# A gated linear attention with a PReLU MLP: small gate operations and the state's decay on other engines, in a new order

## The chip, the core and the metric

The kernel runs on one core of a Trainium2 chip. The core has five engines, each with an instruction queue of its own that it works through in order: TensorE (PE in the profile) for matrix products, VectorE (DVE) and ScalarE (ACT) for elementwise work, GpSimd (POOL) for elementwise work on SBUF, and SyncE (SP), which here issues the transfers between the memory (HBM) and the on-chip SBUF. Matrix products land in PSUM. The metric is the time of one execution in microseconds (us); a change of the kernel is judged by the median of several runs.

## What is computed

The first half is an attention with a complex gate. Each of 4 x 8 heads keeps a state of 48 x 48 complex numbers, which turns and shrinks at every token by a gate per row and takes in the product of key and value; the output reads it with the query. The second half is an MLP with a PReLU on the 3072 tokens.

```python
def _attn_ref(q, k, v, a_re, a_im):              # q, k, v, a_re, a_im: (4, 8, 768, 48)
    mag = np.sqrt(a_re * a_re + a_im * a_im)
    scale = np.minimum(mag, 0.999) / (mag + 1e-06)
    a_re_n, a_im_n = (a_re * scale, a_im * scale)
    for t in range(S):
        ar, ai = (a_re_n[:, :, t, :, None], a_im_n[:, :, t, :, None])
        new_re = ar * S_re - ai * S_im
        new_im = ar * S_im + ai * S_re
        kv = np.einsum('bhd,bhe->bhde', k[:, :, t], v[:, :, t])
        S_re, S_im = (new_re + kv, new_im)
        y[:, :, t] = np.einsum('bhd,bhde->bhe', q[:, :, t], S_re)

def _moe_ref(x, w_in, w_out, alpha):             # x: (3072, 384), w_in: (384, 2048)
    h = x @ w_in
    g = np.maximum(h, 0.0) + alpha * np.minimum(h, 0.0)
    return g @ w_out
```

## The kernel before

The gate of a token is split into a magnitude (the decay) and a direction (the phase). With phases multiplied up along the tokens, keys and queries can be turned once and the state needs only real decays; the decays of a block of tokens are multiplied up in a tree.

**Gates.** `gates(g, b, c0, c1)` does this for batch `b` and the chunks `c0` to `c1` of 128 tokens. There are nine calls, in the list `GATES`: batch 0 in three (1, 2 and 3 chunks), batches 1 to 3 in two of three chunks each. They are numbered g = 0 to 8; the "first gate" is g = 0, "gate 1" and "gate 2" are the other two of batch 0. Rows are the 384 pairs of head and column, as 3 groups of 128 partitions. A call loads the gate (L255), makes the magnitude and its inverse (L263 to L323), the decays (L380) and their tree of products (L396, halving each time; a memset at L383 clears its end), and stores the decays to HBM (L401). The phases are multiplied up in three levels: seven products inside groups of eight tokens (`product`, L416 and L418, on 128x576 and 128x288 elements, later on smaller ones), seven products inside groups of eight of those (the same lines, on 128x72 and 128x36 for three chunks, 128x48 and 128x24 for two), and then the **recurrence**: one product for each of six (or four, or two) remaining blocks, on only 12 and 6 columns, from the value carried over from the gate before (`run`, `carry`, L454 to L468). ScalarE copies the factors between the levels (`three`, L444 and L446). Then the offsets are worked back down (L477, L480), brought to length one (L486 to L492), and multiplied into all tokens by VectorE (L507, L510). The phases are stored to HBM (L502, L512).

The choice of engine for the small steps is made by `tiny`: VectorE in the first gate, GpSimd in the others. `small(k)` and `on(k)` use it for products of up to 80 columns and VectorE for wider ones. For the recurrence `tiny` is set to VectorE in all gates (L454, L455) and set back after it (L468).

**Weights.** The MLP's weights come as 64-bit numbers and are brought to 32 bits in 16 pieces by `to_f32`: ScalarE reads a piece (L588 to L592), GpSimd clips it (L596), VectorE shifts and adds (L598, L600).

**Units.** `unit(u)` does one chunk of one batch, 24 in all. It needs keys and queries (L657, L659), the phases (`PP`, L665) and the decays (`T`, L672), gathered from HBM. VectorE turns keys and queries (L742, L744). Then six levels of halves (1, 2, 4, ... 32 tokens) follow: TensorE multiplies keys by queries (`meet`, L759), VectorE multiplies both by the decays of the next level (`step`, L797), ScalarE copies halves together (L820, L836) and masks results (L773), VectorE too (L782). TensorE transposes the keys (L868), makes the sums of key and value (L880) and the outputs (L900). The **state** `St` is taken along in two halves of 64 tokens: it is multiplied by the decay and the new sum is added by VectorE (L918). In the units 0 to 3 the multiplication is one VectorE instruction of 96x384 (L910), in later ones eight ScalarE instructions of 96x48, one for each head (L916). The state is read by the queries (L930), and the chunk's result goes to HBM (L944, L949).

**MLP.** Groups of one or two chunks are loaded back (L962) and go through `features` (L978, ReLU on ScalarE L985, PReLU on VectorE L987) and `outputs` (L997); the last three groups go through a form with fewer products (`late_features`, `late_outputs`, L1097 to L1172).

**Order.** All of these are Python generators. The string `ORDER` holds one letter for each step: A to I are the gates 0 to 8, J and L the loads of units and values, K spread copies of the values, M start values and weight loads, N and O the weight pieces, P to m the units 0 to 23, n the loads of the MLP, o the MLP, p and q its late form. `plan.run(ORDER)` takes the next step of the task that a letter names, and so writes the queues of all engines in this order; nothing is reordered later. A step waits on its engine for what it needs, and all that stands behind it in the queue waits too.

Of the kernel before, what the change touches and what calls it, by code (L numbers as in the profile page):

```python
# [27 lines left out]


ORDER = (  # L30
    "AABBJAMAJAAAAAAAAAAAJAAMAAAABAJAAAAAABAAAMMMAALALBABAABAABAAANAAAABALAAKOBLNABMNNKAAOMNKABNKBLAALBBK"
    "AOOALABBNABAKAABAKAONMAAKANNAAAABMAOLBAKBOKABABKAAAABLAABANBAAAAOABABABABAKAAKANAAAAANKANBKANAAAOONA"
    "BABLBBNBCBCBKBJBJBBBNBBBOOBCBBBBOBBBCPBOPPJMLLKKBCLCJPCPMOOBBOPPBKOPBBCMKBPNLJBBPPJBCBPNBBCPPNNPBBPK"
    "PJCMBBBCPCPCCPOPBBBBBPOPPBPBOBBMBOBCCCBBBLPBPPPPCPBCCBBPCBPBCPCBOPCPNPOLCCCCDDJCCPCNNNNNCOLCOPLCOOJP"
    "JCPPPCLCDOKCDCNJDCQPPPPCDLMODPNDQMDCNDNKPQJLCQQDLCQNNLQCLOCDQCCCQLCCMDCJDDNQLJOLOOCCCnCJQQCCJDDODQOC"
    "LDKOoJoOoQJDOOQCoCQRDooooCQDLLRQJoQKCooCQQQQQJDMoKCRQQQKoCKNRRQRCNCQOoCQRoQNCRNQCoCoORMQKCoCDCoCoRQo"
    "QLooRQLooCCCCDoLRQoRDLCooRCLoOoCoLRoRJCQCLoooooOQQLQRDCCLoQQCoQRDRDoDNLooLooCCRRCRLRRRLRoooooRoCRKLo"
    "oooooQOOCCCQLooooRooRCDCKoooooDNQDRDRNRRDNJREOoNEDJDNNJoDJRoDLRLDoRDRRRJDoDRoJNDSJDDoDREoooooSDNEJDK"
    "SEDLSESDoSRRRooRESDLLoODonoSSDoSDoooJSTSDELSJoSDoLoLooooSSDoLDDoSLLoooSLTSJSSSoooooSJEooooLoTSLDSLDE"
    "oSJTJooooSoTSTEoKEJooSoSoDTooEDooSTTDSoEEoSTSSEoLELTToLSLoooooSoLDSLELDLSooSoooSoTLSDooSDTSSSoSooKDE"  # L40
    "oLDoooooJEoDDDJooDoTToLoDDDToLELoooooTUoJTDDDDLDTTEKTTJToooooTUDLoDEJoooooUKDoTTnToooJoUEoDToUoTUEoD"
    "UoooETUoEDUDEoEDDTEoKoDooTDoTTLooLoDDooooDLoLooooDLoLoToooDoULoLEULoTLooUUoTEoLUoUJoUFoTTooFTULoTToT"
    "EUoUTTETUUUULUULUoooooEUoVUEoooooUVVUJoEFJoooooJEUoEJUUEUoUUEoLFULoEoJVoELUoFVUJJooLoVEoUKFUVEVLUoEV"
    "UKEoLooooUEVVoUEEoVEooooVoJWVFELVLVoEJooooLoEVVEnEoVJFELoooooLVEWoVELLVVVVFLVLoooooVVVEWJoEJoooWoFKW"
    "EVWJoEWVoFFoooVooooJoEWWEooooFEoEEWVEVWEEVEFVEFVWLVWoLEXLELWEoELoooooLoWWLVFLWEEEEELooooooLoFEWVLEWL"
    "KEEVVVLWWoWWLWVVWoooooVoFVVLWVoEEooWoEWFoWJoFoJoEEWoooJEFooFWEWWEEWJWoLELoWooooEooFWEXLoWLXJJoooXWoF"
    "ooooWWXWXWGoFWXJWLoooooLXXoGoXWWLooooXFoFoFXFoXFFooXooXXoYooGoonoXLooJGYoJXXoLFGXLXLXFXXLXGXLLoooooo"
    "XoGFFLXooooooFXFoGJoooYJXoJoGFKoFXYFoXFXXFXXFXoYXLYoLYJoLYoXXXJYFLGXLFoooooYLXXXXooooXYGoLFoFKYoYGFY"
    "FJoooJoFYYoFLZoFKoGLYFLGoooooJYFZFYLoJYYoFYLYYYJZYFJooooooLZYFGZFLYZLoJZGFooYoYoZoFFZoFFGYoYZYYYYFoZ"
    "oLFYLoFGYLooLFoFFLFYYoYLFGZYLZYYooYYGGFoYFFLFZoFLFoFFoLaoJFFJoooZZoLFGZLJGanoooooGFLFoooZZooZZZFooGZ"  # L50
    "ZLFZGZLFJoooZoGFoZaGFoFoooGZGFoZoaoFZZFZZZZoFFLaoaLFLLFLooooooFoZLoooZaJooLoaLoGaLooooGoaHoHZZaLZGoa"
    "LZaooJGaLoLoGJoaaoaoZZZZoooaZoGaKHGoooaLaoHKGoGHoooooGaoaHaaJaaaJboHoooaooGaoHaGbbKJaoaHaGaooaLGLoHL"
    "ooLGboGbLGoLabJGooooGoLHHGbbLoHbLaGJaobbJooKoGHbGJooLHobLGbabLaabaaGoaLooooGbbLoGLoGbJGoHJooobJGcboJ"
    "obbGbbJbbobGoHoobobocoobobJoHooobGcbbbHbbccLconbHLGcboLooGLcGJcGGLbHGLGcLoGLoooooobcbGoKGcGbGcobobcb"
    "bLGoGHbdoLoGGGHodGoJJooooccKoGcoLoKGHGLHLGoooccocccLGoJoHdLGHJGcoJcooooocoHdGHccGGdoHdcGGooooocoGGoc"
    "GooocoocKcGcccocGodcLoLLKocccooocLddoLocodooodHooHIoIdLdodLoJcoooLHoLoddoJHdoLcooooHdILdoHcLoHLddILo"
    "cIooooooeLdKdodIddddJHJoooododJHoIdHeodIdHdddHLooJHoLoHoeLHoILdJoIHeLHLoooodooeeoeHoLLeoHeLoooHHodLH"
    "oeHLodJoedoHJIeIHLeoLdeIoHKoLedoHneoHHdHeddodIKoooooILeeoeeeeoJIoooJoIHJeeeeoKeoIJHoJfHooeoeooHeIeHf"
    "IeeeeIIofLLoHIJoooeoLHofHHLoeHHfHJIfLfLoLHeeeffKeooooLeofeeeoLoHLHHHoooHfeIfofHHHoofHLoogJHJHfLoHfoo"
    "oooKHIoLHoooLoHIfHJIooKgoIfoffffIffHffHooooJHoLooIoofofgofHogofooooHoooIHfHoJfHffffHgLgLoogLoHofLogg"  # L60
    "oLIoLfoooLgoJooLffoILgfILgfgofJofIfgooggoooIoffogLLoooooLIgJgoggggLoJggIJgooogoIgoIogIogooIogIhgIggg"
    "ghhJJnJoLoLhoJggoLhIgILggoooLhIIghLIghIoghIogoLhhIILIohJILoooooohILihoIhJhLILooooJohhoILiIIoJJIhLJoo"
    "ooooiLooooihIhIoihhiohohJhhoiooIhhoohIoIiihIohioohIiIIIohIIohIIjhhhoLLoIIIhLoIjhoLoILiiLiIoLILhhhIiL"
    "hiIooooLohioIhhhLoIoooIpohoLoIiLiLiioiiLiiJiooooJIioJioIoooioiIoiIIiiiiiijLiJLLjiiioooLooooJIonjjIoo"
    "jILooooJijjooooLijiLoLooooojoLjoJjooLjLoLojjoLoiLoioooijoLoojJojooJjjjjjoJjjJokoJopjojooojojokojkjjk"
    "jjokjLokoLkLokLokojJokjLLLoLkoooooojJkokLjkLjLooLkkoLjkjLojoooojlkjokjkkkkLkkkoooookokoJooolJkokooko"
    "okkkkkoLLolJooJoklJokJoooLooLokJlolLklLkLkookpokkkokoLolloJoooloLoLomlJooolloloolooooomolooooLolLLmL"
    "noooooolLmlomlmlllllooolpooololooomlopooolmmooooomoloomlllllmLmoLmLomomolomolooopooomomllommlollomml"
    "oloomooooooLoooLooomomLoLooLooooloooooLmqLooLoooLooLooooLolonooooomoooooooooooooooooooooooooooopoomo"
    "moooooooomomomoomoomomoopooommomoqmqmqmmmqqmoqqqoooqoooooooqoqqoqooqoqqoooooqqqqooqooqoooooqqoqqoqoo"  # L70
    "qooooooooooqqoooooqqoqqoqooqoqooqoooqqooooqoooooqoqqoqooqoqqooqoqoqqqooqooooqqoooooqoqqoqooqoqooqooq"
    "oqoqooqoqoqoooqqqoqqonoooooooooqqqoqooooooooqoqqqoooooooooooqoqqqoqoqoqqoooqoqqoqooqoqoooooooooooooo"
    "qqoqqoooooooooooqooqoqooooqoqqqoqooqoqooooooooooooooqoqqqoooooooooooqoooooooqoqqoqooqoqqooqoqoqqqoqo"
    "ooooooqqqoooqoqqoqooqoqooooqoqoqooqoqoqoooqqqoqqoooooooooooooqqoooqoooqoqqoqqoooooooooqoooooqqoooqoq"
    "qoqqoooooooooooooooooqooooooooooooqoqqooqooooqoqqqoqooqoqoooooooooooqoooooooooooooqqqoooooqooooqoqqo"
# [1185 lines left out]
```

## Time and profile before

| what | us |
|---|---|
| median of 3 runs (lowest, highest) | 834.2 (831.7, 834.34) |
| the profiled execution | 834.89 |
| its span, first to last instruction | 833.2 |
| TensorE busy in it | 685.4 |
| VectorE busy | 691.2 |
| ScalarE busy | 502.7 |
| GpSimd busy | 249.5 |

The profile is one execution. "Busy" is the time in which an engine worked on an instruction of its own; a wait is put down to the instruction that released it. A group of instructions is given by line, engine, operation and shape: partitions x elements. The page cuts the span into 40 slices of 20.8 us and gives the busy share of each in tenths.

### The profile page before, as it was taken

The numbers are of one execution on the slowest core, as the hardware profiler recorded it, in microseconds if no ns is written. First come the engines' busy times: TensorE is split into PE (matmuls) and PEld (weight loads), VectorE is DVE, ScalarE is ACT, GpSimd is POOL, SyncE is SP. The second block draws the span as 40 slices with busy tenths as digits, with TensorE's granted clock in tenths as the row PEclk, the third lists the DMA queues.
The fourth block names the chain that finished last, engine by engine and source line by source line (L and its number), as shares of the span: only waits on it lengthen the run. The fifth ranks groups of instructions, "written<-read, shape, count | busy, mean of one in ns | idle before, by whom it ended". The sixth has DMA issues, their size and how long they took to land.

```text
span 833.2 us, 27790 instructions
## 1 busy us (share of the span) xinstructions
PE 685.4 (82%) x11680; PEld 542.5 (65%) x11680; DVE 691.2 (83%) x1151; ACT 502.7 (60%) x1243; POOL 249.5 (30%) x341
## 2 busy tenths in 40 slices
PE   0001316859999999899999999999999999999997
PEld 0001315646777667667777777776777777899997
DVE  6978989999999889899998999997887585556574
ACT  8848777557657767776876589554755645311121
POOL 7457454651503110233043121402300000323432
PEclk9999755979999999999999999999999999999999
DMA  7794885696678559547975779678476631201000
GB/s 210 224 274 121 251 233 163 194 217 162 154 226 195 149 145 261 152 123 214 247 177 156 233 165 208 179 193 189 96 204 146 158 90 36 61 2 39 1 20 20
DMA packets 186597, 130.98 MB, mean 157 GB/s; under 512 B 74728, under 2 KB 176872, under 8 KB 186088
## 3 DMA queue, kind: packets, MB, share of 16 engines
q1 hardware_dynamic: 186472, 129.20, 58.5%
q8 instruction: 92, 1.51, 0.8%
q14 instruction: 33, 0.27, 0.1%
HBM read 100.82 MB, written 35.71 MB: 164 GB/s over the span
## 4 chain that ended last, share of the span: by engine, by line
PE 62%; DMA 13%; DVE 11%; SPq 4%; ACT 4%; POOL 4%; issue 2%; DVEq 0%; ACTq 0%; POOLq 0%
PE ps_o L997 18%; PE ps_h L978 16%; PE ps_m L1172 6%; PE ps_lv L759 4%; PE ps_h L1097 3%; PE ps_y L1097 3%; PE ps_y L900 3%; PE ps_kv L880 2%; DVE KQ L797 2%; PE ps_y L930 2%; DVE gate L507 2%; DMA T<-decs 2%; DMA ysc<-T 2%; DMA VL<-in_v_dram 1%; DMA g_sb<-in_w_out_dram 1%
## 5 line engine op out<-in xcount | busy, mean ns | idle before, releaser
L978 PE MATMUL ps_h<-xT,w_in_sb 128*128 128x256 f32 (+1 forms) x960 | 227.8, 369 | 2.8 <-DMA xT<-ysc 1.8
L997 PE MATMUL ps_o<-w_out_sb,g_sb 128*128 128x384 f32 x576 | 224.7, 505 | 5.2 <-DVE g_sb L987 5.0
L978 PEld LDWEIGHTS ps_h<-xT,w_in_sb 128*128 128x128 f32 x960 | 173.0, 196 | 54.9 <-issue 3.2
L797 DVE TENSOR_TENSOR KQ<-KQ,T 96x1024 f32<-96x1024 f32 x120 | 148.8, 1241 | 25.4 <-PE ps_lv L759 18.1
L997 PEld LDWEIGHTS ps_o<-w_out_sb,g_sb 128*128 128x128 f32 x576 | 101.8, 191 | 45.6 <-DVE g_sb L987 7.6
L985 ACT ACTIVATE g_sb<-ps_h 128x256 f32<-128x256 f32 (+1 forms) x160 | 58.0, 362 | 84.7 <-PE ps_h L978 84.1
L759 PE MATMUL ps_lv<-WQ 96*32 96x32 f32 x2304 | 34.9, 204 | 81.7 <-DVE WQ L742 63.0
L416 POOL TENSOR_TENSOR gate<-gate 128x72 f32<-128x72 f32 (+1 forms) x56 | 43.1, 770 | 177.6 <-ACT gate L446 166.1
L759 PEld LDWEIGHTS ps_lv<-WQ 96*32 96x32 f32 x2304 | 26.6, 116 | 101.2 <-DVE WQ L742 63.4
L987 DVE SCALAR_TENSOR_TENSOR g_sb<-g_sb,al,ps_h 128x256 f32<-128x256 f32 (+1 forms) x160 | 71.4, 446 | 20.6 <-ACT g_sb L985 20.4
L1160 POOL TENSOR_TENSOR sums<-g_sb 128x128 f32<-128x128 f32 x48 | 21.9, 476 | 182.0 <-DMA VL<-in_v_dram 109.0
L916 ACT ACTIVATE St<-St,T 96x48 f32<-96x48 f32 x288 | 68.7, 325 | 6.1 <-DVE St L918 6.1
L820 ACT COPY WQ<-KQ 96x1024 f32<-96x1024 f32 x48 | 50.0, 1042 | 23.2 <-DVE KQ L797 23.2
L596 POOL TENSOR_SCALAR top<-top 128x768 f32<-128x768 f32 x16 | 42.6, 2668 | 28.4 <-ACT top L588 26.1
L900 PE MATMUL ps_y<-A,VL 64*48 64x64 f32 x2304 | 42.2, 222 | 8.3 <-issue 6.6
L477 POOL TENSOR_TENSOR gate<-gate,runs 128x252 f32<-128x252 f32 (+1 forms) x16 | 21.0, 1311 | 86.4 <-ACT runs L446 60.5
L507 DVE TENSOR_TENSOR gate<-gate 128x1152 f32<-128x1152 f32 (+2 forms) x36 | 44.3, 1263 | 2.9 <-POOL gate L492 2.7
L416 DVE TENSOR_TENSOR gate<-gate 128x576 f32<-128x576 f32 (+3 forms) x70 | 45.3, 647 | 1.3 <-ACT gate L446 0.4
L900 PEld LDWEIGHTS ps_y<-A,VL 64*48 64x48 f32 x2304 | 39.3, 123 | 10.4 <-issue 9.6
L836 ACT COPY W<-KQ 96x512 f32<-96x512 f32 x48 | 30.8, 642 | 23.7 <-DVE KQ L797 17.4
L759 PE MATMUL ps_lv<-KQ,W 96*32 96x32 f32 x1536 | 24.6, 205 | 24.3 <-ACT W L836 24.0
L773 ACT ACTIVATE A<-ps_lv,columns 128x64 f32<-128x64 f32 x144 | 37.7, 338 | 9.5 <-PE ps_lv L759 9.1
...
## 6 DMA issues: line engine op xcount, KB each, us to landing
...
```

The source lines that it names most:

```text
L416: on(4 * k).tensor_tensor(out=m, in0=w[:, 1::-1].unsqueeze(2).to_broadcast([P, 2, 2, k]), in1=pairs_of(u), op=ALU.mult)
L507: TT(out=m[:, a], in0=U5[:, 1 + a], in1=turned(off3, o)[:, a].unsqueeze(1).unsqueeze(3).to_broadcast([P, L // 2, nb, 2]), op=ALU.mult)
L759: nc.tensor.matmul(t[64 * i + j:64 * i + j + HC // 2, p], lhsT=keys(n, g), rhs=queries(n, g), start=True, stop=True)
L797: nc.vector.tensor_tensor(out=x, in0=x if x0 is None else x0, in1=m, op=ALU.mult)
L820: nc.scalar.copy(z.rearrange("p i n t -> p i (n t)").rearrange("p i (m h) -> p m i h", h=h), bass.AP(tensor=KQ.tensor, offset=KQ.offset + ...
L900: nc.tensor.matmul(o, lhsT=Vp[h][64 * i:64 * i + 64, s, e_ * D:(e_ + 1) * D], rhs=a, start=False, stop=False)
L916: nc.scalar.activation(St[:, n], before[:, n], AF.Copy, scale=T[0:D2, n, TL - 4 + s:TL - 3 + s])
L978: nc.tensor.matmul(p, lhsT=w_in_sb[:, f // 2, kk, f % 2 * P:(f % 2 + 1) * P], rhs=x_of[m][:, kk], start=(kk == 0), stop=(kk == NK - 1))
L985: nc.scalar.activation(gt, p, AF.Relu, scale=-1.0)
L987: nc.vector.scalar_tensor_tensor(out=gt, in0=gt, scalar=al_1[:, f:f + 1], in1=p, op0=ALU.mult, op1=ALU.add)
L997: nc.tensor.matmul(sums[0], lhsT=gt[:, c * P:(c + 1) * P], rhs=w_out_sb[:, f], start=(f == 0), stop=(f == NF - 1))
L1097: nc.tensor.matmul(o, lhsT=lhs, rhs=rhs, start=(at in (0, 5)), stop=(at in (4, 8)))
```

## The change

Three assignments to engines are changed, and the string that sets the order is another one.

- `tiny` is VectorE for the gates 0, 1 and 2 (all of batch 0), and GpSimd for the gates 3 to 8.
- The recurrence no longer goes to VectorE by itself: it is made by the engine that `tiny` names, so by GpSimd in the gates 3 to 8.
- The state is multiplied by the decay on ScalarE in all units; the branch with VectorE's L910 is never taken.
- `ORDER` holds the same steps in another order.

```diff
 ORDER = (
-    "AABBJAMAJAAAAAAAAAAAJAAMAAAABAJAAAAAABAAAMMMAALALBABAABAABAAANAAAABALAAKOBLNABMNNKAAOMNKABNKBLAALBBK"
+    "AABBMMAAAAAAAJAAJAAJAAAAAAAABAAAAAAABAAMMMMAAABABAABAKAABAKANAAAAABAKANBKNNAABOMJBAAAOANOOANBMAKNAAK"
...
-        tiny, tiny_engine = (DVE, nc.vector) if g < 1 else (POOL, nc.gpsimd)
+        tiny, tiny_engine = (DVE, nc.vector) if g < 3 else (POOL, nc.gpsimd)
...
         t = yield from three(ends, blk[:, :, Rn - 1], 2 * rows, t, (R["run"],))
-        here, here_engine = tiny, tiny_engine
-        tiny, tiny_engine = DVE, nc.vector
         t = yield tiny(10, t, *[("carry", g - 1)] * (not first))
...
             done["carry", g] = yield tiny(10, t)
             tiny_engine.tensor_copy(carry, run[:, :, :, nr])
-        tiny, tiny_engine = here, here_engine
         t = yield from three(runs.rearrange("p r (t n) -> p r t n", t=NK), run[:, :, :, 0:nr], 2 * rows, t)
...
-            if u < 4:
+            if u < 0:
                 k_ = yield DVE(H * D, known, takes=(R["St"],))
```

Counted over the whole kernel: VectorE has 1109 instructions in place of 1153, ScalarE 64 more of L916, GpSimd 382 in place of 346; those of TensorE and the 756 transfers of SyncE are the same.

More of the change, by code (lines that the diff above doesn't have):

```diff
@@ L30 @@
 ORDER = (
-    "AABBJAMAJAAAAAAAAAAAJAAMAAAABAJAAAAAABAAAMMMAALALBABAABAABAAANAAAABALAAKOBLNABMNNKAAOMNKABNKBLAALBBK"
[L32 to L75, printed above, removed]
@@ L76 @@
-    "qooqoqqooqoqqqqqqqqqqqqqqqqqqqqqqqqqqqqqqqq")
+    "AABBMMAAAAAAAJAAJAAJAAAAAAAABAAAAAAABAAMMMMAAABABAABAKAABAKANAAAAABAKANBKNNAABOMJBAAAOANOOANBMAKNAAK"
+    "BOKAOAANLAKOALANNBKABLAAAOAKBKOOAAMLAAAKABAAMAABLAAALAAAABAABAABAABAABAAAAAAKBABAAABABANBNBBNONBONNC"
+    "BCOJBNOLBLOOBLBNJBBBBBCBOPCCBPPJMLJJBKNCMBNLBPCBBPCBOCBBBPPCNNPBMBCCJKCBPLCKBPPBCOBCCBCBBOOOBPMBLPPB"
+    "BCLPKBCCKBBBPLJBPKBBBBPBKBBCKPKBPNBPBBBPBBPBPPBPBPPPBPPBPBBCKPBBPNBPKPCNPONLCLNNCCOPDCNJCDOPJPJCCCNC"
+    "LNPPPJCPOMCNCJQOOCNNQJPDCCDLOPCPDQJDQQQLODMQDPQQCDQMDPQQJOQNLOQOOKLQLDDKQODCOnJOLOJLDDQRQLoOOLCoLDoD"
@@ new lines @@
+    "KQoLooJoQoLoDQJQQQMQQooooKCoQDCJCoQCoooooDDQCRoQCRDCRoooooQRCNQoDRONCoooCRoNooCRRCooooQQNNCQCoRLoLCR"
+    "LCoooooRCDCLoCQCLCooRCDoKCoRoLoLRRLCCCCLooooooCMCLCCoooooQKCRCLCLCoCQRLDRCDooLCDLCDRCRoRDRRCRCRRQQRC"
+    "OCRCCoCCRQOCRQQOoCQoQRCCRJRRRQCOOCDCQRLNRLDNKoNDNRRoooREDNNEDoLRDoJRORJDJooooDoJNoRDLNDLDODEnooooJDJ"
+    "SELDSDDEDJSDREJSSRSLoESDLLoooLDSSoDLoDESDoJTLSSDELSJSDoKoooLSSDoJDoDSDoooTDSoSoooLoSSKDSDSJDSSTDJoSK"
+    "ooSoSooTDESJDToTEEDSEoooooSDDoDSEEDooDTDEoooSToDSDSSoDEoLLoooTJSLEoDLDSoooooLTLKoSSSTLoooooTSETDDDDD"
@@ new lines @@
+    "LSoSSSooooTSDooDooooTTooDooooToJDoJooooULoTEEoTLEooJUoonoLTTDTTToELoooooLEToDTooLoTLoUToJoDEUoooooUE"
+    "JUETKEETDDDoJEoooooUoooToDTTKTUUTDUoooLoLDoLUTLooooDoLUULDoLooooDoULoLooooLoUULoTLUTLLoooooUJEUFoETT"
+    "TooEooUUUTTTUTToTFoEUUEUoooUoUEoEoVEooUoUooUoEUVVJJUUUUooLELFUUJoEoLFVoEJUFVJJoEUJVoooooLUEVoFVLUULE"
+    "EUooooFEUVoELooooEVVoEoEFVJELoVooooJEVWFEVnoJVoELLooooEoLVVEEoLVEJoooooKEWVEEVoEWJEJoooooWELVWEVWoLV"
+    "LVFVVVooVoVoooEoFEJFWoEooVoVooEWWoEEVEoWEFVVVEWVFFWLWXKVLWLLoooooEoEVELEWoVLEoooELooKEoLEWELELFFFVWE"
@@ new lines @@
+    "LoLooVVooVoVLFVoEVWVEWVEWFFLLoEEWWWJWWooooooJWWEoWJFJooooEJooWoEWooJEoFooEoWoEWWWoEWWXoKoWXoWooooLFL"
+    "FLoXooooJoFWLoFXFGoXFLWXLWGooLXXoWoXWoWWWoWYXFoooXXoLXooXXonoLXGLFJGoooooXJXFoLXXXLXoGFLYJoooooooFJX"
+    "GXXLLFGooooXooFXFoGFFoooooooGFooXoFoFXooooFJXFJGFXFoXFXYFXXLooJYFoXFKYFXYFLoFYFLooLYoFLYFooFXXLXFYFo"
+    "LXXoXGXXoYXoKYoYGLFooYoFFJFoYYFoFJZFoGLYLFoGLoooooFJZFYJYoYYLFoKYYoooYFYJZoFYYLoGLZoZLYZKoZGFJJoooYF"
+    "KZoFYFoGZoYFGFoFFYYoYZYYoLFLoYLZoFaZYLZFoLZoLFLoYFZZLFoooYoFLYZooYLFoYoFYLGZoZLYFaGYYZZZZGLLGLoooooo"
@@ new lines @@
+    "FFZoJZZZFJZGJoooooZoFZoooZFFZZZZZFoLLoFoJooaFLooooaJoGoLZaonGaZooLaoLoHaoaLoZZHoGZGGLZGZGGaoooLaoGaZ"
+    "LGZaoJaoJoZaaGoooooGHZoLaoHGoooaaGoLGoooaaaoaaLoLaGHooooGoaJHaoJaoJGHooaoGoaboHoaGoaHbbJJaaaaooHLLoJ"
+    "oGoGLboGbLGoKHbJHLooooobLGbaaHGKbGoLobLbGoooGLoGbKoGoLaoLGbboGHHLGboLaobaGaoaaLobbaGoKGobLGGHGoooobG"
+    "bGJoGbbbGJobbbcbGooobobGHobGooboJcoGJbooGbHGbbbbcoGLLobcGJoHboJoLHLGGbbbcJocGGboKbGbLbGLocGbobcocooH"
+    "cJoJcdLGHGLoooooccdJoHGLcnoGLLooooooccoLcGLHLJoooooocdoJcKHdJoooGccdGccdGcocLHcoGHocodcHooooHGoHocoG"
@@ new lines @@
+    "cooocoGGoccGcccoLcoLoGLocHGLooodLdcccooLodLoLooodHIocdIdLodLoLodcdJHoooocodccocLoHooddHodddddodoLoHL"
+    "HoLdIJHooodoHJodeoIdHodoooHoIoHoedoIdddddHILHneHLHHJoooooeoHdLIHeHeLHedHLLHLHodddHLHooooHeeooooHKHoe"
+    "HILLooooeoJIHoLeoedJHoodHJdeHodLoeJeoLoIIddeLHoIooooooHHeHoeHIIHJooHeoHLIJoIoJeHeoeJeeeeKfeHoJfJHooo"
+    "eoeooHHeoHHoHeeHeHeeoLeHLIoeLoofLoHLoIHfJLeLHooeeffoLfIIeHeoeoffoeefoeHLgfooooJgoooofofIJIooofoKoLon"
+    "oILoooffKoHoILofLooooJgooHoKIgfIofIgLIgHHffffffLfooooKHoJfogIfJoKggooofoHfoofoHoJHffffffoLgfLoLoHoLo"
@@ new lines @@
+    "gLfoLHLoooogHgfLgfLofgLfogILfgffLoIoooooooofgIoJgLgggggLggIJIJoooooogIoKgooIogIohgoogIoghhJggggIooLI"
+    "LogJoIoJIgJghLoIghgJogLIooogLoIhoILoIIghoIhgoIoLhILoohhJIoiIoLJhILLihILoLoooooohohILhIJJooooIhhoLIoI"
+    "JhoIIiIooooooohiIJhIiIhhhJoIhhohooIhhIohIIoIIoIhihoiIIhIoIihoIhhIhhihoLILoihLooLjoLIhhhiLIioLIhiohoI"
+    "LhihhoIIhoLioiLojLoLiJoooooLoIioiLooLiiiiiJioiIIoJioiJIoioioooIijiiiiioLoIIIoLoLjiLooooiIoLoLjjJoiiL"
+    "jiIiioooijiiiojooooLojJLoooojoJoLjoJjoojJoJojjJoLojLoLooooLjLjojjjjojjokJjnooooJokojokjooojojokokoko"
@@ new lines @@
+    "jkjkjjjjkjojLkLoLookLjoJkokLjkLjLjoojkLokLojokLjojolLLoookokookkkkjokLolLokLkJpJoookokookokpoookkkkk"
+    "kkoLkolLoLnlJooooooLkoJoLoooJooLlJlklJkollpkkkkkokLooooooolLLmlJJoooooololLmLoooLloLoooooollolooooLm"
+    "LmoooooomllmllooloollplllooloolomlmmoooooomlopmlloooooolllllmLmLolllLmlLlloooLmoLooomoooomooonlooooo"
+    "ooopooooooLmmLomoLooLoLooLoooLooLmoooooomolmoqooooooomommooooopoooooooooooopooomomoooooooooooooooomo"
+    "moooooooomomomoommmooooomooomomoqmqmqmmmqlqmqqqqooooqooqqqoooooqoqqqooooooooqoqqooooqoqqqooooqoqqoqo"
@@ new lines @@
+    "oqooooooqooqqoooooooqoqqoqoooooooooooooooooqonqqqoqooqoqooqoqoqqqqqqqqoqoqqooooooqoooqoqqoqoqooqooqo"
+    "oooqoqooqqooqooqqqoqqoooooooooooooooqqoqoooqqoqoqqoooooooooooooooooqoqqoqooqoqoqqoooooqqoooqooqqoooq"
+    "oqqqooooooooqoqoqooooqooooqoqqqoooooooooooooqoqooooqoqqoqqoooooooooooooooooqoqqoqooqoqooqqqoqoqqqoqo"
+    "oqqooooooooqoqoooooooooqooooqoooooooooooooooqqqooqooqooqooqqqqqqoqqoooooooooooooooooqqqqqoqqqqoqqoqo"
+    "oooooooqoqqqooooqooqoooqoqqoqooqqoooooooooooooooqoqooooooooooooooooooqoqqoqooqqooooooooqqqoooqooooqo"
@@ L79 @@
+    "qqqoqooqoqooqoqqqqqqqqqqqqqqqqqqqqqqqqqqqqq")
 class Ring:
```

## The prediction

> **What bounds the kernel now.** I read the page's first two parts first, then busy time by stage, then who VectorE waits for, then single instructions of GpSimd.
>
> ```profile
> span 833.2 us, 27790 instructions
> PE 685.4 (82%) x11680; PEld 542.5 (65%) x11680; DVE 691.2 (83%) x1151; ACT 502.7 (60%) x1243; POOL 249.5 (30%) x341
> PE   0001316859999999899999999999999999999997
> DVE  6978989999999889899998999997887585556574
> ```
>
> TensorE and VectorE have almost equal work, but not at the same time: TensorE is nearly empty in the first five slices and full from about the ninth on, VectorE is full from the second slice to the 27th. The table by stage gives it in numbers (columns: stage, its length, busy time and count of TensorE, weight loads, VectorE, ScalarE, GpSimd, then clock and DMA).
>
> ```profile
> 14.00:240.00 226.00, 108.04 (x2368) 85.45 (x2368) 206.42 (x338) 152.75 (x280) 113.35 (x98) 0.87 0.72 202
> 240.00:380.00 140.00, 131.78 (x2397) 97.94 (x2396) 124.96 (x184) 102.65 (x259) 28.82 (x45) 0.99 0.67 174
> 380.00:640.00 260.00, 256.77 (x4827) 193.06 (x4826) 235.55 (x334) 172.62 (x480) 54.63 (x77) 1.00 0.73 187
> 640.00:834.00 194.00, 188.78 (x2093) 166.02 (x2091) 118.00 (x274) 63.06 (x200) 43.35 (x96) 1.00 0.19 50
> ```
>
> From 380 us to the end TensorE is idle for 3.2 + 5.2 us, partly because the last slice is cut short. So the time is made of TensorE's work, which the change leaves alone, and of its idle time before 380 us: 14 + 118 + 8.2 us. In that lead-in VectorE is busy for 206.4 of 226 us, so what is worth something is VectorE's work ahead of the early units and its waits there. The waits of VectorE between 14 and 240 us (total, times, longest):
>
> ```profile
> DVE top L598 <- POOL top L596: 7.1, 3, 3.8
> DVE gate L507 <- POOL gate L492: 2.7, 1, 2.7
> DVE g_sb L987 <- ACT g_sb L985: 2.2, 4, 1.0
> DVE WQ L742 <- DMA PP<-phs: 1.7, 1, 1.7
> ```
>
> Of its 19.6 us idle, 9.8 us are GpSimd's fault: the weight pieces (L596) stand in the same queue as the small gate operations and are late. Why those operations take long is seen in the second gate's chain (start, duration):
>
> ```profile
> 51.76 0.28 POOL L416 TENSOR_TENSOR gate<-gate 128x48 f32<-128x48 f32 x1
> 52.12 0.23 POOL L418 TENSOR_TENSOR gate<-gate 128x24 f32<-128x24 f32 x1
> 52.44 0.29 POOL L416 TENSOR_TENSOR gate<-gate 128x48 f32<-128x48 f32 x1
> 52.80 1.16 POOL L418 TENSOR_TENSOR gate<-gate 128x24 f32<-128x24 f32 x1
> 54.04 2.50 POOL L416 TENSOR_TENSOR gate<-gate 128x48 f32<-128x48 f32 x1
> ```
>
> The same form takes 0.28 us, and 2.50 us once VectorE's 1.2 us rotations (L742 at 52.65, L744 at 53.91) run beside it.
>
> **The change, part by part.**
>
> *Small operations of gates 1 and 2 to VectorE.* VectorE has no row for most of these sizes; its neighbours (128x48 at 0.208, 128x24 at 0.184, 128x96 at 0.255, 128x192 at 0.355, 128x288 at 0.476 us) bracket each within 0.05 us. Gate 1: 14 products 2.7, decay ends (L396) 0.6, L477 and L480 1.1, L488 to L492 0.9: 5.3 us. Gate 2: 3.0 + 0.6 + 1.4 + 1.0 = 6.0 us. VectorE gets 11.3 us more before 240 us. GpSimd loses about 22 us of gate 1 (rows 5.7, 4.2, 4.4, 5.3 and small ones) and 19 us of gate 2 (a seventh of 131 us, the rows of seven like gates). With that the 16 weight pieces of 2.67 us stand alone in GpSimd's queue, so I take the waits of 7.1 and 2.7 us as gone. If that cover is wrong, because ScalarE brings the pieces late (GpSimd waited 26.1 us for L588), they stay: bounds 0 and 9.8 us, and I take 9.8, since the causes named were L596 and L492 themselves.
>
> *State times decay.* Eight VectorE instructions (L910, mean 0.599) go: 4.8 us less. ScalarE gets 64 more of L916 at 0.325: 20.8 us, between about 80 and 240 us, where it is busy for 106.6 of 160 us (127.4 then). Queued behind them are ScalarE's copies for the units (L820, L836), for which TensorE waits already. The multiplication needs only the earlier state and the decays, so it can run before the new sums are there; where it can't, a half costs 8 x 0.325 - 0.6 = 2.0 us more. In the trace TensorE waits directly for the state's sum (L918) two times, 6.0 us. Bounds: 0, and 8 halves x 2.0 = 16 us; I take 1 us, nearer to the lower end, as six of eight halves had nobody waiting.
>
> *The recurrence of gates 3 to 8 to GpSimd.* VectorE loses per gate 6 x 0.171 + 6 x 0.165 and a copy or two of 0.245, 2.3 us; 13.6 us in six gates, 2.3 of them before 240 us. GpSimd has no row of 12 or 6 columns. Its 128x12 decay row is 0.208 us alone, its 128x36 product 0.594 us on average and up to 1.25 when it collides, so 12 operations cost from 2.5 to 15 us; I take 7. Behind them in GpSimd's queue stand only the same gate's L477 to L492 and the next gate's memset and L396. On ScalarE the copy L444 to `runs` waits, and in VectorE's queue L507. What hides the chain is VectorE's other work between a gate's last large product (L418, 128x288) and its first L507. Summed from the mean rows in the program order of each kernel, scaled by 691.2/749.8 because neighbouring rows overlap, that cover is 49, 36, 37, 40, 40, 34 us before and 40, 34, 35, 37, 38, 27 us after for gates 3 to 8. The chain is 14 products 9.5 (7 x 1.36), recurrence 7, tail 6.4, ScalarE's hops 3.2: 26 us. It fits, in gate 8 by nothing. I cost it at 0.
>
> The Trainium skill (SBUF — State Buffer, Who interferes with whom) says that a VectorE instruction with two SBUF inputs and a GpSimd instruction that reads SBUF shut each other out for the whole instruction. The 0.28 and 2.50 us above agree; by that rule each of the 12 could wait out a whole rotation, which is the first rival.
>
> *The order.* All 756 transfers of the SP queue remain. Gate 1's decay store goes from the 37th to the 41st place, behind gate 0's phases, some 2 us by issues of 0.4 to 0.6 us; gate 1's phases (L512) from 75th to 76th, unit 1's gather of them (L665) from 80th to 83rd. Unit 1 meets its phases with 11 us of VectorE rows between, against about 10 us from L510 to the gathered tile before: just in time, 0. For VectorE I summed the rows ahead of each unit's first rotation (L742): scaled, they grow by 1.6 us for unit 1, 0.5, 8.9, 6.9, 3.7, 5.2, 4.0, 1.7 for units 2 to 8, then shrink by 1.4 (unit 9), grow by 2.0 (10), shrink by 3.5 (11). These sums already hold the three parts above.
>
> *The sum.* VectorE reaches a unit earlier by the 9.8 us of waits less that growth: unit 3 by 0.9 us, 4 by 2.9, 5 by 6.1, 6 by 4.6, 7 by 5.8, 8 by 8.1, 10 by 7.8. TensorE's idle time ends to grow somewhere between unit 6 and unit 10, so it can shrink by about 6 us. Less the 1 us of ScalarE: 5 us. The profiled execution took 834.9 us (span 833.2 and 1.7 around it); 834.9 - 5 = 829.9. Its time lies 0.7 us over the median of the runs, 834.2, so I say 829.
>
> **The rivals.** *The GpSimd chain becomes the wait (slower).* Place: L507 of gates 4, 5 and 8. With the colliding prices (14 products 13.4 as in gate 3, 12 operations at 1.0, tail 9.8, hops 3.2) the chain is 38 us against 34, 35 and 27 us: 4 + 3 + 11 us of VectorE standing still, and behind L507 stand L987 and the units, with two `ps_h` buffers of cover, so perhaps two thirds reaches TensorE, 12 us: 829 + 12 = 841 us. It decides when an operation of the recurrence costs over about 0.7 us. For it: many of the rows at 1.2 us. Against: gate 8's products ran at 0.26 to 0.32 us.
>
> *ScalarE becomes the bound of the lead-in (slower).* Between 80 and 100 us it is busy for 16.1 of 20 us; 16 instructions of unit 0 make 21.3. If half of the eight halves pay 2.0 us and the copies behind lose as much again, 16 us less the gain: 834.2 + 16 - 6 = 844 us. Against: 20% of the stage stays free.
>
> *Nothing to measure.* The waits on GpSimd are replaced by waits for transfers, whose share is 0.72 in the lead-in (the gather of decays at 99.5 us took 6.6 us): unit 3, which gains only 0.9 us, then sets the rest, 834 us. That the change does not do what it says can be ruled out: the counts of the rows follow the text.
>
> **How the numbers follow.** What a measurement here can tell from no change is about 0.3%, 2.5 us. Forecast 0.48 (its own range 821 to 833), GpSimd's chain 0.22, ScalarE 0.15, nothing 0.15. Faster: 0.44 of the forecast and 0.02 of nothing, 0.46. Same: 0.04 + 0.10 + 0.02 + 0.02 = 0.18. Slower: 0.20 + 0.13 + 0.03 = 0.36. The range goes down to 834 less all of the 9.8 us and half of the 8.2 us idle from 240 to 380, 820, and up to both slower cases, 846.
>
> **What would show it.** Right: between 14 and 240 us no wait of VectorE for L596 or L492 over 1 us in total, VectorE busy there by some 4 us more, TensorE's idle time before 380 us down from 140 to about 135 us, L507 without waits. Wrong: waits of L507 for L492 of several us at gates 4, 5, 8; waits of L918 or of the units' matmuls for ScalarE that grow by more than 5 us; or VectorE's gaps filled by DMA waits at L742 and L797.

## The result and the profile after

The changed kernel took 822.98 us (median of 4 runs, 821.21 to 826.72), the kernel before 833.93 us beside it (4 runs, 831.70 to 834.34): a ratio of 0.9856, 95% interval 0.9821 to 0.9892. It is faster by 11 us; 5 us were forecast. The same kernel on another chip gave 0.9864 (0.9820 to 0.9907; run e11 below). The chips differ by up to 0.5% (the kernel before took 833.9, 835.0, 837.0 and 838.4 us on those used), so runs are compared here by their ratio to the kernel before on the same chip, and traces by the times inside them. The profiled execution of the changed kernel is one of its slower ones, 826.7 us.

In the changed kernel the lines behind the recurrence are numbered 2 or 3 lower: L742 is now L739, L797 is L794, L916 and L918 are L913 and L915, L987 is L984, L507 is L504.

From the first two parts of the page after the change:

```profile
span 825.0 us, 27851 instructions
PE 694.1 (84%) x11680; PEld 548.3 (66%) x11680; DVE 684.1 (83%) x1107; ACT 519.3 (63%) x1307; POOL 268.2 (33%) x377
PE   0001439859999999998999999989999999999997
DVE  5999999999998999896989988978777786455574
```

VectorE's row of nines now holds from the second slice to the 12th; before, the third, fourth and sixth slices were at 7 and 8. Over the whole kernel VectorE works 7.1 us less, ScalarE 16.6 us more, GpSimd 18.7 us more. By stage (columns as in the prediction's table of stages):

```profile
14.00:240.00 226.00, 122.41 (x2492) 96.62 (x2493) 217.96 (x375) 174.58 (x363) 78.41 (x67) 0.93 0.74 207
240.00:380.00 140.00, 133.86 (x2470) 99.85 (x2469) 125.05 (x153) 102.38 (x263) 53.98 (x75) 0.98 0.73 186
380.00:640.00 260.00, 257.35 (x4812) 192.23 (x4811) 222.14 (x284) 174.29 (x480) 84.36 (x115) 0.99 0.69 178
640.00:834.00 194.00, 180.49 (x1911) 159.64 (x1909) 113.33 (x273) 56.91 (x179) 42.83 (x96) 0.99 0.17 44
```

Between 14 and 240 us VectorE is idle for 8.0 us in place of 19.6, and TensorE gets 124 more of its instructions done. VectorE is busy for 11.5 us more there, not for the 4 us of the prediction's signs: by 240 us it has come further in its queue, to 375 instructions in place of 338. GpSimd's load in that stage fell by 35 us. VectorE's longest waits there (in total, times, longest):

```profile
DVE g_sb L984 <- ACT g_sb L982: 2.3, 3, 1.9
DVE St L915 <- ACT St L913: 0.7, 1, 0.7
DVE gate L380 <- ACT gate L373: 0.5, 1, 0.5
DVE KQ L794 <- ACT WQ L817: 0.5, 2, 0.3
```

The view lists no wait for GpSimd any more (it leaves out waits of up to 0.15 us); before there were 9.8 us of them.

TensorE's busy time is no measure of progress here. Two traces of the changed kernel show it: for about the same work before 380 us (4960 and 4948 instructions) TensorE was busy for 256.3 us in this one and for 245.8 us in e11's, because the same product takes longer in some stretches. L897's 64x64 product took 308 ns on average between 140 and 160 us in this one, at a granted clock of 0.70, and 218 ns in e11's, at 1.00. The row of the clock does not tell it everywhere: between 100 and 120 us it says 0.50 before and 1.00 after, yet the 96x32 product (L759, now L756) took 244 ns in both. The start of each unit's first rotation (L742, now L739) is a better measure. From the traces, in us; the last row is e11, whose chip is 0.5% slower:

| unit | 1 | 2 | 3 | 4 | 5 | 6 | 7 | 8 | 10 | 12 | 16 | 23 |
|---|---|---|---|---|---|---|---|---|---|---|---|---|
| before | 103.64 | 130.86 | 177.02 | 188.27 | 216.57 | 247.74 | 265.00 | 286.90 | 352.37 | 409.51 | 510.85 | 668.66 |
| after | 98.09 | 119.56 | 172.33 | 181.85 | 209.92 | 240.49 | 257.73 | 275.39 | 339.89 | 401.03 | 499.06 | 659.36 |
| earlier by | 5.6 | 11.3 | 4.7 | 6.4 | 6.7 | 7.3 | 7.3 | 11.5 | 12.5 | 8.5 | 11.8 | 9.3 |
| forecast for VectorE | | | 0.9 | 2.9 | 6.1 | 4.6 | 5.8 | 8.1 | 7.8 | | | |
| e11, earlier by | 5.0 | 10.7 | 3.7 | 5.7 | 4.7 | 5.1 | 5.0 | 8.8 | 9.3 | 4.9 | 7.6 | 6.8 |

### The profile page after: what moved, and what is told of

Its sections match the earlier page's. It is cut to its first block, busy times and chain, and to the rows that moved or that the text cites. A ratio compares the mean times of both kernels' runs of the same rounds, so it can differ in the third digit from the quotient of the medians.

```text
span 825.0 us, 27851 instructions
## 1 busy us (share of the span) xinstructions
PE 694.1 (84%) x11680; PEld 548.3 (66%) x11680; DVE 684.1 (83%) x1107; ACT 519.3 (63%) x1307; POOL 268.2 (33%) x377
## 4 chain that ended last, share of the span: by engine, by line
PE 69%; DVE 11%; DMA 10%; ACT 3%; issue 2%; POOL 2%; SPq 2%; DVEq 0%; POOLq 0%; ACTq 0%
PE ps_o L994 21%; PE ps_h L975 20%; PE ps_m L1169 6%; PE ps_lv L756 5%; PE ps_y L1094 4%; PE ps_h L1094 4%; PE ps_y L897 4%; PE ps_y L927 3%; PE ps_kv L877 3%; DVE KQ L794 3%; DMA VL<-in_v_dram 2%; DMA T<-decs 2%; PE ps_kt L865 2%; DMA gate<-in_a_im_dram 1%; DMA KQ<-in_q_dram 1%
## 5 line engine op out<-in xcount | busy, mean ns | idle before, releaser
L994 PE MATMUL ps_o<-w_out_sb,g_sb 128*128 128x384 f32 x576 | 228.0, 510 | 2.5 <-DVE g_sb L984 2.5
L794 DVE TENSOR_TENSOR KQ<-KQ,T 96x1024 f32<-96x1024 f32 x120 | 149.2, 1244 | 28.4 <-PE ps_lv L756 19.5
L756 PE MATMUL ps_lv<-WQ 96*32 96x32 f32 x2304 | 34.5, 204 | 79.1 <-DVE WQ L739 63.2
L756 PEld LDWEIGHTS ps_lv<-WQ 96*32 96x32 f32 x2304 | 26.4, 116 | 98.9 <-DVE WQ L739 63.6
L984 DVE SCALAR_TENSOR_TENSOR g_sb<-g_sb,al,ps_h 128x256 f32<-128x256 f32 (+1 forms) x160 | 71.3, 446 | 24.7 <-ACT g_sb L982 22.7
L913 ACT ACTIVATE St<-St,T 96x48 f32<-96x48 f32 x352 | 83.8, 323 | 3.9 <-DVE St L915 3.8
L416 POOL TENSOR_TENSOR gate<-gate 128x72 f32<-128x72 f32 x42 | 24.2, 575 | 148.9 <-ACT gate L446 146.1
L416 DVE TENSOR_TENSOR gate<-gate 128x576 f32<-128x576 f32 (+5 forms) x84 | 50.7, 604 | 1.1
L897 PE MATMUL ps_y<-A,VL 64*48 64x64 f32 x2304 | 44.7, 229 | 7.5 <-issue 5.3
L897 PEld LDWEIGHTS ps_y<-A,VL 64*48 64x48 f32 x2304 | 41.7, 129 | 9.1 <-issue 6.5
L396 POOL TENSOR_TENSOR gate<-gate 128x72 f32<-128x72 f32 (+2 forms) x18 | 19.1, 1059 | 79.4 <-DVE gate L396 78.5
L941 ACT COPY T<-ps_y 48x256 f32<-48x256 f32 x96 | 31.8, 365 | 18.4 <-PE ps_y L927 17.6
L833 ACT COPY W<-KQ 96x512 f32<-96x512 f32 x48 | 30.7, 640 | 19.5 <-DVE KQ L794 11.4
L504 DVE TENSOR_TENSOR gate<-gate 128x1152 f32<-128x1152 f32 (+2 forms) x36 | 42.9, 1219 | 0.1
L756 PE MATMUL ps_lv<-KQ,W 96*32 96x32 f32 x1536 | 24.1, 204 | 21.3 <-ACT W L833 21.3
```

The costliest lines, as they stand in the source:

```text
L416: on(4 * k).tensor_tensor(out=m, in0=w[:, 1::-1].unsqueeze(2).to_broadcast([P, 2, 2, k]), in1=pairs_of(u), op=ALU.mult)
L756: nc.tensor.matmul(t[64 * i + j:64 * i + j + HC // 2, p], lhsT=keys(n, g), rhs=queries(n, g), start=True, stop=True)
L794: nc.vector.tensor_tensor(out=x, in0=x if x0 is None else x0, in1=m, op=ALU.mult)
L897: nc.tensor.matmul(o, lhsT=Vp[h][64 * i:64 * i + 64, s, e_ * D:(e_ + 1) * D], rhs=a, start=False, stop=False)
L984: nc.vector.scalar_tensor_tensor(out=gt, in0=gt, scalar=al_1[:, f:f + 1], in1=p, op0=ALU.mult, op1=ALU.add)
L994: nc.tensor.matmul(sums[0], lhsT=gt[:, c * P:(c + 1) * P], rhs=w_out_sb[:, f], start=(f == 0), stop=(f == NF - 1))
```

## The experiments

The string of letters fits any mix of the three edits, as each step stays one step whatever engine it goes to. So the parts were taken apart: A is the small operations of gates 1 and 2 on VectorE, B the recurrence of gates 3 to 8 on GpSimd, C the state's multiplication on ScalarE in all units. Ratios to the kernel before on the same chip, with 95% intervals. A difference of two of them is known to about 0.004 or 0.005 only, 4 us:

| edits | old order | new order |
|---|---|---|
| none | 1 | 0.9962 (0.9930 to 0.9993), e1 |
| A | 0.9952 (0.9925 to 0.9980), e4 | 0.9886 (0.9845 to 0.9927), e9 |
| A, B | 0.9887 (0.9855 to 0.9918), e8 | 0.9878 (0.9847 to 0.9909), e6 |
| A, C | 1.0021 (0.9992 to 1.0050), e10 | 0.9863 (0.9832 to 0.9895), e5 |
| B, C | | 0.9943 (0.9914 to 0.9972), e3 |
| A, B, C | 0.9966 (0.9931 to 1.0001), e2 | 0.9856 and 0.9864, the changed kernel and e11 |

### e1: the new order alone

```diff
 ORDER = (
-    "AABBJAMAJAAAAAAAAAAAJAAMAAAABAJAAAAAABAAAMMMAALALBABAABAABAAANAAAABALAAKOBLNABMNNKAAOMNKABNKBLAALBBK"
+    "AABBMMAAAAAAAJAAJAAJAAAAAAAABAAAAAAABAAMMMMAAABABAABAKAABAKANAAAAABAKANBKNNAABOMJBAAAOANOOANBMAKNAAK"
...
```

> The new order with the engines as they were before. Theory A (the gain comes from gates 1 and 2 leaving GpSimd's queue): the waits of VectorE for GpSimd before 240 us stay or grow beyond the 9.8 us of the kernel before, since the new order leaves less VectorE work beside gate 1's chain; 836 to 848 us. Theory O (the order itself is the better one, whatever the engines): 821 to 827 us, TensorE's clock and busy time in 100 to 140 us as in the changed kernel.

Measured 833.4 us against 835.0, ratio 0.9962. Neither theory: the order gives a little without the edits, and far less than the 1.4% of the whole. VectorE's waits between 14 and 240 us in e1:

```profile
DVE gate L507 <- POOL gate L492: 4.1, 2, 2.8
DVE gate L416 <- ACT runs L446: 3.2, 2, 1.9
```

The waits for L596 are gone with the order alone, but VectorE still waits for the gates' chain, 4.1 us directly and 3.2 us through ScalarE's copies, which come after GpSimd's products.

### e2: the three edits in the old order

```diff
-        tiny, tiny_engine = (DVE, nc.vector) if g < 1 else (POOL, nc.gpsimd)
+        tiny, tiny_engine = (DVE, nc.vector) if g < 3 else (POOL, nc.gpsimd)
...
-        here, here_engine = tiny, tiny_engine
-        tiny, tiny_engine = DVE, nc.vector
...
-        tiny, tiny_engine = here, here_engine
...
-            if u < 4:
+            if u < 0:
```

> The new engines for gates, recurrence and state in the old order. Theory A: the waits of VectorE for L596 and L492 go below 2 us before 240 us and most of the gain is there, 824 to 829 us. Theory O: no gain without the order, 832 to 838 us, because VectorE carries 4 us more before 240 us and the places in its queue are the old ones.

Measured 834.1 us against 835.0, ratio 0.9966, not clear of 1: in the range of theory O. The waits for GpSimd did go, as theory A had it, but most of the gain did not come. VectorE between 14 and 240 us in e2:

```profile
DVE St L915 <- ACT St L913: 6.9, 7, 1.9
DVE g_sb L984 <- ACT g_sb L982: 5.7, 6, 1.9
```

The first line is new: seven times the sum of the state (L915) stands waiting for ScalarE's multiplication, because the old order has the two steps side by side, which did for VectorE's 0.6 us but not for eight ScalarE instructions of 0.32 us (e10 takes this edit by itself).

### e3: the changed kernel without A

```diff
-        tiny, tiny_engine = (DVE, nc.vector) if g < 3 else (POOL, nc.gpsimd)
+        tiny, tiny_engine = (DVE, nc.vector) if g < 1 else (POOL, nc.gpsimd)
...
+        here, here_engine = tiny, tiny_engine
+        if g < 3:
+            tiny, tiny_engine = DVE, nc.vector
...
+        tiny, tiny_engine = here, here_engine
```

> The changed kernel, but the small operations of gates 1 and 2 on GpSimd again (their recurrence on VectorE as before). Theory A: VectorE waits for GpSimd at L507 of gate 1 and at L598, 10 us or more in total before 240 us; 834 to 848 us. Theory O: 821 to 827 us. If the recurrence on GpSimd or the state on ScalarE made the gain, likewise 821 to 827 us.

Measured 830.3 us against 835.0, ratio 0.9943. The size is below what theory A expected, but its direction holds: A is worth 0.008 to 0.009 in the new order (0.9943 against 0.9856 and 0.9864). The same 4.1 and 3.2 us of waits as in e1 are there.

### e4: A alone, in the old order

```diff
-        tiny, tiny_engine = (DVE, nc.vector) if g < 1 else (POOL, nc.gpsimd)
+        tiny, tiny_engine = (DVE, nc.vector) if g < 3 else (POOL, nc.gpsimd)
```

> The kernel before with only the small operations of gates 1 and 2 on VectorE, order, recurrence and state as before. Theory A: the waits of 9.8 us go, VectorE's extra 11 us before 240 us eat part of it; 826 to 832 us. Theory O: 834 to 842 us, the extra work of VectorE in a full lead-in shows and nothing pays for it.

Measured 830.9 us against 835.0, ratio 0.9952: as theory A had it. VectorE works 10.8 us more between 14 and 240 us (217.18 in place of 206.42) and is none the later for it, because it stands still for only 8.8 us in place of 19.6: unit 3 begins at 170.66 us, 6.4 us earlier, and unit 6 at 244.84 us, 2.9 us earlier. Its longest waits there:

```profile
DVE g_sb L987 <- ACT g_sb L985: 4.7, 4, 2.1
DVE KQ L797 <- PE ps_lv L759: 0.3, 1, 0.3
DVE KQ L797 <- ACT WQ L820: 0.3, 1, 0.3
DVE gate L269 <- ACT gate L267: 0.2, 1, 0.2
```

### e5: the changed kernel without B

```diff
+        here, here_engine = tiny, tiny_engine
+        tiny, tiny_engine = DVE, nc.vector
         t = yield tiny(10, t, *[("carry", g - 1)] * (not first))
...
+        tiny, tiny_engine = here, here_engine
```

> The changed kernel with the recurrence of gates 3 to 8 back on VectorE. Theory V (time goes with VectorE's work and waits): 13.6 us more of VectorE, 2.3 of it before 240 us; units 12 to 23 begin 2 to 5 us later than in the changed kernel, 824 to 828 us. Rival (the longer chain on GpSimd, 12 operations at a measured 0.88 us, holds something back even in the changed kernel): 815 to 821 us.

Measured 825.4 us against 837.0, ratio 0.9863: no difference from the changed kernel that can be measured. Neither a gain of VectorE's 13.6 us nor a cost of GpSimd's longer chain reaches the end; its units 12 and 23 begin at 401.4 and 657.1 us, the changed kernel's at 401.0 and 659.4. The 825.4 us lie in theory V's range only because this chip is slower; by the ratio it would be 822.5 us on the first chip, between the two ranges.

### e6: the changed kernel without C

```diff
-            if u < 0:
+            if u < 4:
                 k_ = yield DVE(H * D, known, takes=(R["St"],))
```

> The changed kernel with VectorE's multiplication of the state in units 0 to 3 again. Theory V: 4.8 us more of VectorE before 240 us, all units from 4 on 3 to 5 us later, 825 to 829 us. Rival (the 20.8 us more of ScalarE cost as much as VectorE saves): 820 to 824 us, no difference; if ScalarE is the dearer, 815 to 820 us.

Measured 826.3 us against 837.0, ratio 0.9878: 0.002 above the changed kernel, inside both intervals. By the ratio that is 823.8 us on the first chip, in the range of "no difference". In the new order C is worth nothing measurable either. Up to unit 6, which begins at 243.1 us, VectorE works for 221.5 us here and for 218.2 and 217.4 us in the two traces of the changed kernel; it stands idle for 7.6 us here and for 8.3 and 11.3 us there. So C takes 3 to 4 us of work off VectorE and gives 1 to 4 us back in waits.

### e7: the recurrence made twice on GpSimd

```diff
-        def product(dst, u, w, m, k, t):
+        def product(dst, u, w, m, k, t, times=1):
...
+            for _ in range(times):
...
-            t = yield from product(run[:, :, :, j + 1], ends[:, :, :, j], run[:, :, :, j], f, NK, t)
+            t = yield from product(run[:, :, :, j + 1], ends[:, :, :, j], run[:, :, :, j], f, NK, t, 1 if g < 3 else 2)
```

> The changed kernel with every product of the recurrence of gates 3 to 8 made twice on GpSimd: 12 more operations of some 0.88 us in each chain, 10.5 us, on no other engine. If the cover counted in VectorE's rows (27 to 40 us) is all there is, the chain of 37 us overruns it in gates 4, 5 and 8 by 3, 2 and 10 us and L507 waits for L492: 830 to 840 us. If VectorE's own waits and the time between its rows widen the cover, L507 waits for less than 5 us in total and the time stays at 821 to 826 us.

Measured 845.4 us against 837.0, ratio 1.0115 (1.0074 to 1.0156): 0.026 above the changed kernel, 21 us. That is more than the first alternative expected, and its mechanism did not come: VectorE waits nowhere for L492. The added operations also cost less than the 0.88 us each that was expected. GpSimd's two groups of the recurrence:

```profile
L417 POOL TENSOR_TENSOR gate<-run,runs 128x12 f32<-128x12 f32 x72 | 42.1, 585 | 18.3 <-ACT runs L448 13.1
L420 POOL TENSOR_TENSOR run<-gate 128x6 f32<-128x6 f32 x72 | 37.9, 527 | 5.6
```

In the changed kernel the 36 and 36 of them took 32.5 and 30.5 us, so 72 more operations added 17 us. From its first start to its last end a chain takes 15.2 us on average, in place of 11.4: 3.8 us were added to each gate, not 10.5. One of the waits of ScalarE, in total and the one of gate 3 in order of time:

```profile
ACT runs L446 <- POOL gate L417: 20.7, 6, 4.6
```

```profile
204.16 0.22 ACT L446 COPY runs<-run 128x36 f32<-128x36 f32 x1 [4.59 <-POOL gate L417]
```

L446 is `three`'s copy behind the recurrence (L444 before), L417 the product. In each of the six gates ScalarE stands still for 3.5 us on average, with the units' copies and the ReLU queued behind it: VectorE's waits for ScalarE at L987's line rise from 22.7 to 36.8 us, at L918's from 7.8 to 13.3 us. In the changed kernel this wait is 1.1 us once (in e11 2.5 and 1.1 us). Collisions with VectorE are not the cause: VectorE's own work did not grow (683.0 us busy, 684.1 in the changed kernel). So the chain's cover is what ScalarE has to do between two of its own copies, not what VectorE has before L507: of the 3.8 us added to a chain 3.3 us stuck out (20.7 less 1.1 us, over six gates), so the changed kernel's chain had only about half a microsecond to spare on average (an estimate from one trace of each kernel).

### e8: A and B in the old order

```diff
-        tiny, tiny_engine = (DVE, nc.vector) if g < 1 else (POOL, nc.gpsimd)
+        tiny, tiny_engine = (DVE, nc.vector) if g < 3 else (POOL, nc.gpsimd)
...
-        here, here_engine = tiny, tiny_engine
-        tiny, tiny_engine = DVE, nc.vector
...
-        tiny, tiny_engine = here, here_engine
```

> The old order with gates 1 and 2 on VectorE and the recurrence of gates 3 to 8 on GpSimd, the state as before. In the old order the three edits together took 834 us, 3 us more than the first alone, with 6.9 us of waits of L918 for ScalarE's L916. If the state on ScalarE is what the old order can't take: no such waits before 240 us and 825 to 830 us. If it is the recurrence: waits of L507 for L492 after 240 us and 832 to 836 us.

Measured 827.7 us against 837.0, ratio 0.9887, with no wait of L915 between 14 and 240 us, as expected if the state on ScalarE is what the old order can't take. With A and B the old order does as well as the new one (0.9878), so nearly all of the change can be had without a new order, if C is left out.

### e9 and e10: A in the new order, A and C in the old one

e9 is e4's edit with the new order, e10 is e4's edit and `u < 0` in the old one.

> The new order with only the small operations of gates 1 and 2 on VectorE; recurrence and state as before. If VectorE's work and waits set the time, this is the changed kernel with 13.6 + 4.8 us more of VectorE: 0.990 to 0.994 of the kernel before, and the first edit is worth 0.003 to 0.006 in the new order (0.9962 without it). If the new order pays only together with the recurrence and the state, 0.995 or more.

> The old order with gates 1 and 2 on VectorE and the state on ScalarE, recurrence on VectorE. If the state on ScalarE is what the old order can't take: L918 waits for L916 by 5 us or more before 240 us and the ratio is 1.000 to 1.006, worse than the first edit alone (0.9952). If those waits cost nothing at the end: 0.991 to 0.996.

e9: 829.9 us against 838.4, ratio 0.9886; A is worth 0.0076 in the new order, more than expected, and A with the new order alone is all of the change but 0.002 to 0.003, which is inside the noise. e10: 839.9 us against 838.4, ratio 1.0021, as expected if the old order can't take C: C in the old order takes back A's gain and a little more. VectorE between 14 and 240 us in e10:

```profile
DVE St L918 <- ACT St L916: 7.0, 7, 1.8
```

### e11 and e12: the changed kernel again, and the state on GpSimd

e11 is the changed kernel as it is. In e12:

```diff
-            if u < 0:
-                k_ = yield DVE(H * D, known, takes=(R["St"],))
+            if u < NU:
+                k_ = yield POOL(H * D, known, takes=(R["St"],))
...
-                nc.vector.tensor_tensor(out=St, in0=before, in1=T[0:D2, :, TL - 4 + s:TL - 3 + s].to_broadcast([D2, H, D]),
+                nc.gpsimd.tensor_tensor(out=St, in0=before, in1=T[0:D2, :, TL - 4 + s:TL - 3 + s].to_broadcast([D2, H, D]),
```

> The changed kernel on this chip, to stand beside the other three: 0.982 to 0.989 of the kernel before.

> The changed kernel with the state's multiplication as one GpSimd instruction of 96x384 in all units: ScalarE loses 352 x 0.325 = 114 us, GpSimd gets 44 instructions; its 128x288 product took 0.88 us, so 1.0 to 1.5 us each, 44 to 66 us. If ScalarE's queue is what VectorE and TensorE wait for next (22.7 us of L984 for L982, 7.8 us of L915 for L913 in the changed kernel): 805 to 818 us, ratio 0.965 to 0.982. If GpSimd's reads shut out VectorE's two-input instructions, or its queue makes the state late behind the gates' chains: 825 us or more, ratio above 0.987, with waits of L915 for L907.

e11: 829.2 us against 838.4, ratio 0.9864. e12: 837.2 us against 838.4, ratio 0.9983 (0.9956 to 1.0009), 0.012 worse than the changed kernel beside it, although ScalarE is busy for 440.9 us in place of 518.8. GpSimd's costliest group in e12 (count, then busy time and mean in ns, then its idle time before):

```profile
L907 POOL TENSOR_TENSOR St<-St,T 96x384 f32<-96x384 f32 x44 | 66.4, 1509 | 154.0 <-DVE St L915 119.7 <-PE ps_y L927 18.4 <-DVE run L418 7.9
```

The in-order queues fit this: the multiplication waits in GpSimd's queue for the sum of the half before (119.7 us in all), the gates' chains stand behind it, and VectorE (L915 for L907 10.8 us) and ScalarE wait in turn (L483 for GpSimd's L477 14.9 us, 0.3 in e11). VectorE's rows also got longer, 694.4 us in place of 683.5 for the same instructions. How much of the loss is the one and how much the other was not separated. No version here is measurably faster than the changed kernel.

## Why the prediction was right, point by point

**What bounds the kernel.** Right in the main: VectorE's waits in the lead-in set the time. The edit that ended them made the kernel faster (A, in both orders), and the one that brought new ones took that back (C in the old order). Less work for VectorE did not do it by itself: in the new order C and B, which both take work off VectorE, gave nothing measurable (e6, e5).

**Small operations of gates 1 and 2.** Here two terms of the sum were mis-sized. The price was forecast as 11.3 us, and the rows of the changed kernel do add up to 12.3 us (14 products 3.2 and 3.6, L474 and L477 2.9, the ends and the rest 2.6). But neighbouring rows overlap, and e4, which has this edit alone and the old order, shows what it takes of VectorE's time. VectorE from 14 us to the start of unit 3, before, in e4 and after:

```profile
14.00:177.02 163.02, 54.16 (x1295) 44.04 (x1296) 146.37 (x246) 110.07 (x178) 88.75 (x73) 0.84 0.72 211
```

```profile
14.00:170.66 156.66, 52.55 (x1296) 42.43 (x1296) 153.44 (x294) 110.44 (x178) 40.91 (x25) 0.87 0.76 221
```

```profile
14.00:172.33 158.33, 62.40 (x1302) 49.46 (x1302) 154.04 (x292) 126.64 (x235) 46.32 (x27) 0.93 0.76 217
```

In e4 VectorE's work grew by 7.1 us, not 11.3, and its idle time fell by 13.4 us, not 9.8. In this stretch of the kernel before VectorE waited 9.8 us for GpSimd and 4.2 us for transfers, ScalarE and TensorE; in e4 the view lists no wait at all. So the waits that the prediction had left as they were went with this edit, and it needs no new order for that. After the whole change the work grew by 7.7 us (8.9 forecast) and the idle time fell by 12.4 (in e11 by 7.0 and 10.7): unit 3 begins 4.7 us earlier (e11: 3.7) in place of 0.9. Up to unit 6 it is 5.2 us of work, as forecast, against 12.5 us of idle time (e11: 4.4 and 9.5). The forecast then took "about 6 us" for the shift of units 6 to 10, which was 7.3 to 12.5 us in one trace and 5 to 9 us in e11's.

That the forecast came as near as it did is partly luck. In its own terms this edit takes more of VectorE than it gives back (11.3 us, or 10.4 with the scaling of its sums, against 9.8), and the gain comes from the 4.8 and 2.3 us that C and B take off VectorE before 240 us. The runs show the opposite: this edit is worth 0.005 in the old order and 0.008 in the new one, 4 and 6 us, and in the new order C and B nothing measurable.

**State on ScalarE.** 1 us was taken, with bounds of 0 and 16 us. In the new order e6 shows no difference in time; the waits of L915 for L913 before 240 us are 0.7 us in one trace and 3.3 us in e11's, so the 1 us is neither shown nor refuted, and the 4.8 us that VectorE is spared do not show in the time either. In the old order the edit costs 0.007 to 0.008, 6 us (e10 against e4, e2 against e8). That the price hangs on the order and not on the operation was not in the prediction.

**Recurrence on GpSimd.** 7 us for a gate were taken; its 72 instructions took 903 and 847 ns on average, 10.5 us for a gate. It was costed at nothing, and cost nothing that can be measured (e5). The chain of gate 3, alternating products and sums of 12 and 6 columns:

```profile
188.23 1.14 POOL L416 TENSOR_TENSOR gate<-run,runs 128x12 f32<-128x12 f32 x1 [2.48 <-ACT runs L446]
189.45 1.20 POOL L418 TENSOR_TENSOR run<-gate 128x6 f32<-128x6 f32 x1
190.73 1.34 POOL L416 TENSOR_TENSOR gate<-run,runs 128x12 f32<-128x12 f32 x1
192.14 1.29 POOL L418 TENSOR_TENSOR run<-gate 128x6 f32<-128x6 f32 x1
193.51 0.23 POOL L416 TENSOR_TENSOR gate<-run,runs 128x12 f32<-128x12 f32 x1
193.82 1.20 POOL L418 TENSOR_TENSOR run<-gate 128x6 f32<-128x6 f32 x1
195.09 0.23 POOL L416 TENSOR_TENSOR gate<-run,runs 128x12 f32<-128x12 f32 x1
```

The reason given, that VectorE's rows before L507 (27 to 40 us of them) cover a chain of 26 us, looked at the wrong queue, as e7 shows: the chain is first missed by ScalarE's copy. By the prediction's count gate 3 had 14 us to spare and gate 8 nothing; by the estimate from e7 it was about half a microsecond on average. So that the cost of nothing came true was luck. The rival's place was wrong too, and its threshold of 0.7 us for an operation was passed without any wait of L504.

**Where the 11 us come from.** A is worth 0.005 in the old order and 0.008 in the new one; the new order is worth 0.004 by itself, 0.007 with A, 0.016 with A and C, 0.011 with all three, and 0.001 with A and B. In the old order B is worth 0.0065 beside A (e8 against e4) and 0.0055 beside A and C (e2 against e10), and in the new one nothing measurable. Why the new order and B can each give the second half of the gain but not add up is not settled. It fits that TensorE is nearly full from 380 us on in all of these kernels (1.2, 3.4 and 2.7 us idle up to 640 us in e5, e4 and the changed one), so that work taken from VectorE later than that has nothing left to buy; but no run was made for that.

**The rivals.** ScalarE as the bound of the lead-in did not come true in the new order; in the old one its sign, waits of L918 for ScalarE, came (7.0 us in e10). Waits for transfers did not take the place of those for GpSimd: T at L794 0.2 us between 14 and 240 us. TensorE's idle time before 380 us, forecast at 135 us, was 123.7 us in one trace of the changed kernel and 134.2 us in the other, so this sign cannot tell a gain of 5 us.
